# Linear attention and a gelu layer: the bf16 cast of v split between VectorE and ScalarE

## The chip, the cores and the metric

The kernel runs on one core of a Trainium2 chip. The metric is the device time of one execution in microseconds (us), the median of several runs. The core has five engines with a queue each: TensorE (PE in the profile, with PEld for its weight loads), VectorE (DVE), ScalarE (ACT), GpSimd (POOL) and SyncE (SP), which issues most DMA transfers. Each engine works through its own queue in order. They wait for one another through semaphores.

## The reference

Linear attention over 8 batches, 8 heads, 576 tokens and a head size of 64 makes a matrix of 4608 tokens by 512. This goes through two matrix products with a gelu between.

```python
def phi(x):
    return np.where(x > 0, x, np.exp(x) - 1.0) + 1.0
q_p, k_p = (phi(q), phi(k))
kv = np.einsum('bhsd,bhse->bhde', k_p, v)
z = np.sum(k_p, axis=2)
num = np.einsum('bhsd,bhde->bhse', q_p, kv)
den = np.einsum('bhsd,bhd->bhs', q_p, z)[..., None] + 1e-06
x = num / den                      # 4608 x 512 after moving the heads inside
h = x @ w_in                       # 512 -> 2048
g = 0.5 * h * (1.0 + np.tanh(c * (h + 0.044715 * h * h * h)))
out = g @ w_out                    # 2048 -> 512
```

All inputs and the output are float32. The kernel casts to bf16 for TensorE.

## The kernel before

The work goes batch by batch. For batch b there are these stages.

- k and v are loaded as `[128, 4, 9 * 64]`: a pair of heads `u` (four of them) fills the 128 partitions, 64 to a head, and each partition holds nine tokens, J = 9, of 64 values.
- `exp_of` (ScalarE, L219), `linear_of` (VectorE, L227) and `least_of` (VectorE, L233) compute phi of q and k in bf16 as the smaller of exp(x) and max(x + 1, 1).
- `cast_v_paired` (L237 to L241) casts v to bf16 into `vp`, in which the token `j` is outside the pair `u`, and each head's 64 values are followed by a one, so that the product with k gives the sum of k as a 65th column. Before the change it is one VectorE instruction for a whole batch (L238, 2304 elements a partition), and for batch 0 two, one for each half of the pairs.
- `kv_paired` (L243) multiplies k by v on TensorE: nine tokens, two pairs `s` and two head parities `a` make 36 small matmuls for one half of the pairs. `kv_evac` (L258) copies the sums out of PSUM into the block diagonal tile `kvbd`.
- `transpose_q` turns phi of q around on TensorE into PSUM (`t_ps`), and ScalarE copies it into `qts` (L430 in batch 0, L536 in batch 1). From batch 2 on a DMA does this.
- `nab` and its variants multiply q by `kvbd` (`n_ps`) and divide. The result x is transposed into `xt`.
- `h_mm` (L385) multiplies by `w_in`, `gelu` (L395) runs on ScalarE, and `o_mm` (L726) multiplies by `w_out`.

The pool is under a manual schedule, so each engine does its instructions in the order in which the code issues them. Batch 0 is written out in `first_batch`: the maps of q and k, the q transposes, the casts of v, and the two kv products, with `keep_warm` matmuls in between as filler for TensorE. The first product's sums lie in two banks of their own, one for each of two engines to copy; the second's lie in `pair_of_banks`, whose two banks are copied for one half of the partitions by VectorE and for the other by ScalarE (L451).

The attention of batch 1 is placed by `plan_second` into the steps of batch 0's gelu layer. `at(j, slot, fn)` queues a piece to be issued after step `slot` of batch j. The steps 0 to 15 of batch 0 are the sixteen blocks of h. Steps 16 to 35 are the output products, four tiles of tokens side by side over successive blocks of `w_out`. The pieces that matter here:

```python
at(0, 15, maps)
at(0, 23, transpose_q)
at(0, 23, casts)
at(0, 27, kv)
at(0, 27, last_w_out)
at(0, 29, n, 0)
```

Steps 24 to 27 are of two matmuls each, eight in all, and stand on TensorE between the transposes and the kv product. `maps` ends on ScalarE with a cast of half a block of `w_out`, `casts` does the other half on VectorE after v, and `last_w_out` casts the last block on GpSimd and ScalarE in turn.

PSUM is used through two pools: `ps_b` with six banks, from which `bank()` takes `h_ps`, `o_ps`, `t_ps` and batch 1's `kv_ps`, and `ps_a` with one pair of banks. The sum `o_ps` of each of the four token tiles of batch 0 is held from the first block to the last, that is from steps 16 to 19 up to steps 32 to 35.

Of the kernel before, what the change touches and what calls it, by code (L numbers as in the profile page):

```python
# [15 lines left out]
def kernel(  # L16
# [16 lines left out]
    nc = tc.nc  # L33

    B, H, S, D = q.shape
# [6 lines left out]
    NP = H // 2  # L42
    J = S // HP
    KM = d_model // P
    MM = d_ff // P
    E = D + 1
# [32 lines left out]
    def bank(name, shape, dt=FP32):  # L79
        return ps_b.tile(shape, dt, name=name, tag="b")  # L80

    def pair_of_banks(name):
        return ps_a.tile([P, 2, 512], FP32, name=name, tag="a")
# [3 lines left out]
    ld = {}  # L87
# [63 lines left out]
    halves = (slice(0, 2), slice(2, 4))  # L151
# [39 lines left out]
    def vp_paired(b):  # L191
        return vps[b % 2].rearrange("p (j u) e -> p j u e", u=NP)
# [19 lines left out]
    def exp_of(name, b, hs=None):  # L212
        x = ld[name, b]
        hs = hs or slice(0, x.shape[1])
        if (name, b) not in exps:
            e = name + ("_e" if name != "qr" or b % 2 else "_f")
            exps[name, b] = pe.tile([P, x.shape[2] // D, x.shape[1], D], BF16, name=e)
        o, i = maps_view(name, b, x, exps[name, b], hs)
        nc.scalar.activation(o, i, AF.Exp)  # L219

    def linear_of(name, b, hs=None):
        x = ld[name, b]
        hs = hs or slice(0, x.shape[1])
        if (name, b) not in phi:
            phi_tiles(name, b)
        o, i = maps_view(name, b, x, phi[name, b], hs)
        nc.vector.tensor_scalar(o, i, 1.0, 1.0, op0=ALU.add, op1=ALU.max)  # L227

    def least_of(name, b, hs=None):
        p, e = phi[name, b], exps[name, b]  # L230
        if hs:
            p, e = p[:, :, hs, :], e[:, :, hs, :]
        nc.vector.tensor_tensor(p, p, e, op=ALU.min)  # L233

    def cast_v_paired(b, us, fn):  # L237
        fn(  # L238
            out=vp_paired(b)[:, :, us, 0:D].rearrange("p j u d -> p u j d"),
            in_=ld["v", b][:, us].rearrange("p u (j d) -> p u j d", d=D),  # L240
        )  # L241

    def kv_paired(b, ii, kv_of):  # L243
# [14 lines left out]
    def kv_evac(b, blocks, src, *fns):  # L258
        for s in range(2):
            r = slice(HP * s, HP * (s + 1))  # L260
            fns[s % len(fns)](out=kvbds[b][r, blocks, E * s : E * (s + 1)], in_=src[r])  # L261
# [28 lines left out]
    def x_tile():  # L290
        return px.tile([P, d_model], BF16, name="x")
# [120 lines left out]
    def first_batch():  # L412
        w_ps = bank("w_ps", [P, 512])

        def keep_warm(n):
            for _ in range(n):
                nc.tensor.matmul(w_ps, lhsT=warm[:, 0:P], rhs=warm)  # L417

        qt = pt.tile([P, C, NP, P], BF16, name="qt")
        qs = (slice(0, 4), slice(4, 8))  # L420

        def transpose_q(s, fn):
            t_ps = bank("t_ps", [P, C, 2, P], BF16)
            for i in range(2):
                for c in range(C):
                    h = 4 * s + 2 * i
                    nc.tensor.transpose(
                        t_ps[:, c, i, :], phi["q", 0][:, c, h : h + 2, :], ident
                    )
            fn(out=qt[:, :, 2 * s : 2 * s + 2, :], in_=t_ps)  # L430

        keep_warm(18)
        for s in range(2):
            for n, hs in (("q", qs[s]), ("k", halves[s])):
                exp_of(n, 0, hs)
                linear_of(n, 0, hs)
                least_of(n, 0, hs)
        transpose_q(0, nc.scalar.copy)
        keep_warm(8)
        transpose_q(1, nc.scalar.copy)  # L440
        keep_warm(5)
        for ii in range(2):
            cast_v_paired(0, halves[ii], nc.vector.tensor_copy)
        kv_ps = [bank("kv_ps", [P, E]) for _ in range(2)]
        kv_paired(0, 0, lambda a, ii: kv_ps[a])
        for a, fn in enumerate((nc.vector.tensor_copy, nc.scalar.copy)):
            kv_evac(0, slice(2 * a, 2 * a + 1), kv_ps[a].rearrange("p (i e) -> p i e", i=1), fn)
        keep_warm(1)
        kv_ps = pair_of_banks("kv_ps")
        kv_paired(0, 1, lambda a, ii: kv_ps[:, a, 0:E])  # L450
        kv_evac(0, slice(1, 4, 2), kv_ps[:, :, 0:E], nc.vector.tensor_copy, nc.scalar.copy)  # L451
        for fs in (slice(0, 128), slice(128, 256), slice(256, 512)):
            cast_w_in(0, nc.gpsimd.tensor_copy, fs)
        cast_w_in(1, nc.gpsimd.tensor_copy, slice(256, 512))
        for i in range(2, 4):
            cast_w_in(i, nc.gpsimd.tensor_copy)
        for i in range(2):
            cast_w_out(i, nc.gpsimd.tensor_copy)

        xts[0] = pt.tile([P, NP, MAIN], BF16, name="xt")  # L460
        x = {0: x_tile()}

        def t(c, blocks=range(NP)):
            transpose_x(x[c], xt_chunk(0, c), nc.scalar.copy, blocks)

        def h(m, c, blocks=range(KM)):
            h_begin(0, m, slice(P * c, P * (c + 1)), blocks)

        first, second = range(2), range(2, 4)
        nab_half(x[0], qt[:, 0], 0)  # L470
        nab_half(x[0], qt[:, 0], 1)
        x[1] = nab(qt[:, 1], 0)
        t(0, first)
        h_begun[0][0] = bank("h_ps", [P, MAIN])
        nc.tensor.matmul(h_begun[0][0], lhsT=warm[:, 0:P], rhs=warm, skip_group_check=True)
        t(0, second)
        for m in range(2):
            h(m, 0, first)
        x[2] = nab_in_banks(qt[:, 2], 0)
        h(0, 0, second)  # L480
        t(1)
        h(1, 0, second)
        x[3] = nab(qt[:, 3], 0)
        cast_w_in(1, nc.vector.tensor_copy, slice(0, 256))
        h(2, 0)
        h(3, 0)
        t(2)
        for m in range(3):
            h(m, 1)
        t(3)  # L490
        gelu_table()
        h(3, 1)
        for c in (2, 3):
            for m in range(4):
                h(m, c)

    first_batch()


# [12 lines left out]
    def plan_second():  # L512
        b = 1
        x = {}

        def maps():
            for n in "qk":
                exp_of(n, b)
            cast_w_out(2, nc.scalar.copy, slice(0, 2))
            for n in "qk":  # L520
                linear_of(n, b)
            for n in "qk":
                least_of(n, b)

        def transpose_q():
            qts[b] = pt.tile([P, C, NP, P], BF16, name="qt")
            for s in range(2):
                t_ps = bank("t_ps", [P, 2, NP, P], BF16)
                for c in range(2):
                    for i in range(NP):  # L530
                        nc.tensor.transpose(  # L531
                            t_ps[:, c, i, :],
                            phi["q", b][:, 2 * s + c, 2 * i : 2 * i + 2, :],
                            ident,
                        )
                nc.scalar.copy(qts[b][:, 2 * s : 2 * s + 2], t_ps)  # L536

        def casts():
            cast_v_paired(b, slice(0, NP), nc.vector.tensor_copy)
            cast_w_out(2, nc.vector.tensor_copy, slice(2, 4))  # L540

        def kv():
            kv_ps = [bank("kv_ps", [P, 2, E]) for _ in range(2)]
            for ii in range(2):
                kv_paired(b, ii, lambda a, ii: kv_ps[a][:, ii, :])
            for a, fn in enumerate((nc.vector.tensor_copy, nc.scalar.copy)):
                kv_evac(b, slice(2 * a, 2 * a + 2), kv_ps[a], fn)

        def last_w_out():
            for m, fn in enumerate((nc.gpsimd.tensor_copy, nc.scalar.copy) * 2):  # L550
                cast_w_out(3, fn, slice(m, m + 1))
            gelu_table()

        def n(c):
            x[c] = (nab_in_banks if c == 1 else nab)(qts[b][:, c], b)

        def t(c):
            if c == 0:
                xts[b] = pt.tile([P, NP, MAIN], BF16, name="xt")
            transpose_x(x[c], xt_chunk(b, c), nc.scalar.copy)  # L560
# [7 lines that stand above are left out]
        at(0, 29, n, 1)  # L568
        at(0, 32, n, 2)
        at(0, 32, t, 0)  # L570
        at(0, 33, t, 1)
        at(0, 33, n, 3)
        at(0, 34, t, 2)
        at(0, 34.5, t, 3)
        at(0, 35, h_begin, b, 0, slice(0, 3 * P))
        at(0, 35, h_begin, b, 0, slice(3 * P, MAIN))
# [253 lines left out]
```

## Time and profile before

| what | value |
|---|---|
| time, median of 3 runs | 283.59 us (283.57 to 283.64) |
| span of the profiled execution | 281.8 us |
| TensorE busy | 276.0 us, 98% |
| ScalarE busy | 164.4 us, 58% |
| VectorE busy | 102.6 us, 36% |
| GpSimd busy | 15.0 us, 5% |
| casts of v on VectorE (L238), all batches | 9 instructions, 11.0 us |
| kv product of batch 0, second half | from 12.43 us |
| kv product of batch 1 | from 39.68 us |

The busy time of an engine is the sum of its instructions. The chain of waits follows the work that ended last back from the end, at each step to what released it. The timeline lists the instructions of each engine by their start, counted in us from the start of the span. In its rows, what stands in brackets is the idle time of that engine just before and what ended it. A group of equal instructions that follow one another is one row with a count; its duration runs from the first start to the last end.

### The profile page before, as it was taken

The page shows a single profiled execution, that of the slowest core. Times are in us where ns is not written, and L with a number is a line of the kernel's source. Part 1 is how long each engine was busy: PE and PEld are TensorE (multiplying, and loading weights), DVE is VectorE, ACT ScalarE, POOL GpSimd, SP SyncE. Part 2 cuts the span into 40 slices and gives each one's busy share as a digit, 9 for nine tenths or more (in the row PEclk, how much of TensorE's full clock was granted, in tenths as well). Part 3 has the DMA queues.
Part 4 walks back from the last instruction along what each step waited for, and adds up shares of the span by engine and source line. Part 5 has one row for each costly group of instructions (what it writes and reads, how often), then busy time and mean ns, then how long its engine had stood idle before and what let it go on. Part 6 is the DMA issues. An engine that isn't in the chain of part 4 may idle for free.

```text
span 281.8 us, 5145 instructions
## 1 busy us (share of the span) xinstructions
PE 276.0 (98%) x2181; PEld 134.9 (48%) x2181; DVE 102.6 (36%) x177; ACT 164.4 (58%) x224; POOL 15.0 (5%) x21
## 2 busy tenths in 40 slices
PE   8899999999999999999999999999999999999995
PEld 3574455445444544454445444544444444444444
DVE  3850386344955750356034640350124001400001
ACT  4678878785986915692569346833681364026400
POOL 3147210000000000000000000000000000000000
PEclk9999999999999999999999999999999999999999
DMA  6999999978999777906794630056405300420022
GB/s 244 400 406 397 411 401 404 404 256 218 190 367 296 267 170 214 370 24 172 201 385 101 161 120 2 2 149 169 93 2 149 111 2 0 131 94 0 0 77 74
DMA packets 59590, 53.81 MB, mean 191 GB/s; under 512 B 35760, under 2 KB 45360, under 8 KB 59568
## 3 DMA queue, kind: packets, MB, share of 16 engines
q1 hardware_dynamic: 56784, 44.58, 50.7%
q10 hardware_dynamic: 2784, 8.91, 8.9%
q8 instruction: 17, 0.28, 0.4%
q14 instruction: 5, 0.04, 0.0%
HBM read 36.70 MB, written 9.44 MB: 164 GB/s over the span
## 4 chain that ended last, share of the span: by engine, by line
PE 94%; DMA 3%; SPq 1%; DVE 1%; issue 0%; ACT 0%
PE o_ps L726 44%; PE h_ps L385 44%; DMA v_x<-in_v_dram 3%; PE n_ps L323 1%; PE n_ps L249 1%; PE kv_ps L249 1%; PE n_ps L265 1%; PE t_ps L378 1%; SPq L95 1%; SPq L100 0%; PE t_ps L531 0%; DVE vp L238 0%; DVE x L368 0%; DVE kvbd L261 0%; DVE o_sb L687 0%
## 5 line engine op out<-in xcount | busy, mean ns | idle before, releaser
L726 PE MATMUL o_ps<-w_out_sb,g 128*128 128x512 bf16 (+2 forms) x608 | 128.4, 368 | 0.0
L385 PE MATMUL h_ps<-xt,w_in_sb 128*128 128x512 bf16 (+1 forms) x564 | 113.7, 359 | 0.0
L395 ACT ACTIVATE g<-h_ps 128x512 bf16<-128x512 f32 x144 | 84.6, 599 | 36.3 <-PE h_ps L385 35.1
L385 PEld LDWEIGHTS <-w_in_sb 128*128 128x128 bf16 x628 | 58.5, 98 | 64.6
L726 PEld LDWEIGHTS <-g 128*128 128x128 bf16 x608 | 57.4, 98 | 63.5
L687 ACT COPY o_sb<-o_ps 128x512 f32<-128x512 f32 (+1 forms) x19 | 10.8, 576 | 65.4 <-PE o_ps L726 58.6
L687 DVE COPY o_sb<-o_ps 128x512 f32<-128x512 f32 (+1 forms) x19 | 12.2, 645 | 50.4 <-PE o_ps L726 45.5
L282 DVE RECIPROCAL r<-n_ps 128x6 f32<-128x6 f32 (+2 forms) x43 | 8.2, 191 | 61.3 <-PE n_ps L323 55.8
L227 DVE TENSOR_SCALAR k_p<-k_x 128x2304 bf16<-128x2304 f32 (+1 forms) x9 | 11.0, 1222 | 24.1 <-DMA k_x<-in_k_dram 24.1
L283 DVE TENSOR_TENSOR xs<-n_ps,r 128x384 bf16<-128x384 f32 (+1 forms) x30 | 17.5, 584 | 1.0
L219 ACT ACTIVATE k_e<-k_x 128x2304 bf16<-128x2304 f32 (+1 forms) x9 | 17.1, 1903 | 0.9 <-DMA k_x<-in_k_dram 0.8
L219 ACT ACTIVATE q_e<-q_x 128x2048 bf16<-128x2048 f32 (+1 forms) x9 | 15.5, 1719 | 2.8 <-DMA q_x<-in_q_dram 2.7
L227 DVE TENSOR_SCALAR q_p<-q_x 128x2048 bf16<-128x2048 f32 (+1 forms) x9 | 9.9, 1102 | 13.0 <-DMA q_x<-in_q_dram 13.0
L385 PE MATMUL h_ps<-xt_rest,w_in_sb 128*128 128x512 bf16 x64 | 14.0, 379 | 0.0
L233 DVE TENSOR_TENSOR q_p<-q_p,q_e 128x2048 bf16<-128x2048 bf16 (+1 forms) x9 | 9.9, 1099 | 6.9 <-ACT q_e L219 6.8
L408 ACT ACT_TABLE_LOAD x9 | 11.5, 1283 | 0.2
L233 DVE TENSOR_TENSOR k_p<-k_p,k_e 128x2304 bf16<-128x2304 bf16 (+1 forms) x9 | 11.0, 1221 | 1.2 <-ACT k_e L219 1.0
L238 DVE CAST vp<-v_x 128x2304 bf16<-128x2304 f32 (+1 forms) x9 | 11.0, 1222 | 0.5 <-DMA v_x<-in_v_dram 0.4
L417 PE MATMUL w_ps<-warm 128*128 128x512 bf16 x32 | 9.7, 459 | 1.2 <-DVE warm L181 1.2
L219 ACT ACT_TABLE_LOAD x8 | 10.3, 1283 | 0.1
L139 POOL CAST w_in_sb<-w_st 128x512 bf16<-128x512 f32 (+2 forms) x6 | 7.6, 1270 | 14.7 <-DMA w_st<-in_moe_w_in_dram 14.7
L283 DVE TENSOR_TENSOR x<-n_ps,r 128x512 bf16<-128x512 f32 (+1 forms) x13 | 7.9, 609 | 0.4
(50 smaller groups left out, 75.9 us busy)
## 6 DMA issues: line engine op xcount, KB each, us to landing
out_dram<-o_sb ACTq DMA_DIRECT2D x16, 512.0 KB, 3.8
k_x<-in_k_dram SPq DMA_DIRECT2D x7, 1152.0 KB, 7.0
v_x<-in_v_dram SPq DMA_DIRECT2D x7, 1152.0 KB, 12.0
q_x<-in_q_dram SPq DMA_DIRECT2D x6, 1024.0 KB, 11.8
w_st<-in_moe_w_in_dram SPq DMA_DIRECT2D x3, 1024.0 KB, 13.5
q_x<-in_q_dram SPq DMA_DIRECT2D x4, 512.0 KB, 8.4
w_st<-in_moe_w_out_dram SPq DMA_DIRECT2D x2, 1024.0 KB, 12.5
w_st<-in_moe_w_out_dram SPq DMA_DIRECT2D x4, 512.0 KB, 11.2
```

The source lines that it names most:

```text
L219: nc.scalar.activation(o, i, AF.Exp)
L227: nc.vector.tensor_scalar(o, i, 1.0, 1.0, op0=ALU.add, op1=ALU.max)
L233: nc.vector.tensor_tensor(p, p, e, op=ALU.min)
L238: fn(out=vp_paired(b)[:, :, us, 0:D].rearrange("p j u d -> p u j d"), in_=ld["v", b][:, us].rearrange("p u (j d) -> p u j d", d=D),)
L282: nc.vector.reciprocal(r, n_v[heads + (D,)])
L283: nc.vector.tensor_tensor(x_v, n_v[heads + (slice(0, D),)], r[heads + (None,)].to_broadcast(shape + [D]), op=ALU.mult,)
L385: nc.tensor.matmul(h_ps[:, ts], lhsT=w_in_sb[:, c, P * m : P * (m + 1)], rhs=xt[:, c, ts], start=(c == 0), stop=(c == KM - 1), skip_group_ ...
L395: nc.scalar.activation(g[:, m, :], h_ps, AF.Gelu_apprx_tanh)
L408: nc.scalar.preload_act_table_set("gelu_apprx_tanh_and_others")
L417: nc.tensor.matmul(w_ps, lhsT=warm[:, 0:P], rhs=warm)
L687: (nc.scalar.copy if on_scalar else nc.vector.tensor_copy)(dst, src)
L726: nc.tensor.matmul(o_ps, lhsT=g[:, m, P * t : P * (t + 1)], rhs=w_out_sb[:, m, fs], start=(m == 0), stop=(m == MM - 1),)
```

## The change

`cast_v_paired` gets a parameter `js`, the tokens that it casts. In batch 0 the second half of v, and in batch 1 all of v, is cast in two parts: tokens 0 to 5 by VectorE and 6 to 8 by ScalarE. In batch 1 ScalarE's part is issued between its two copies of the transposed q. In addition, both copies of batch 0's second kv product are issued to ScalarE, where VectorE did one of them. What it is for: v lands late in both batches, TensorE's product needs all of it, and two engines share the cast.

```diff
-    def cast_v_paired(b, us, fn):
+    def cast_v_paired(b, us, fn, js=slice(0, J)):
         fn(
-            out=vp_paired(b)[:, :, us, 0:D].rearrange("p j u d -> p u j d"),
-            in_=ld["v", b][:, us].rearrange("p u (j d) -> p u j d", d=D),
+            out=vp_paired(b)[:, js, us, 0:D].rearrange("p j u d -> p u j d"),
+            in_=ld["v", b][:, us].rearrange("p u (j d) -> p u j d", d=D)[:, :, js],
         )
...
-        for ii in range(2):
-            cast_v_paired(0, halves[ii], nc.vector.tensor_copy)
+        cast_v_paired(0, halves[0], nc.vector.tensor_copy)
+        cast_v_paired(0, halves[1], nc.vector.tensor_copy, slice(0, 6))
+        cast_v_paired(0, halves[1], nc.scalar.copy, slice(6, J))
...
-        kv_evac(0, slice(1, 4, 2), kv_ps[:, :, 0:E], nc.vector.tensor_copy, nc.scalar.copy)
+        kv_evac(0, slice(1, 4, 2), kv_ps[:, :, 0:E], nc.scalar.copy)
...
                 nc.scalar.copy(qts[b][:, 2 * s : 2 * s + 2], t_ps)
+                if s == 0:
+                    cast_v_paired(b, slice(0, NP), nc.scalar.copy, slice(6, J))
 
         def casts():
-            cast_v_paired(b, slice(0, NP), nc.vector.tensor_copy)
+            cast_v_paired(b, slice(0, NP), nc.vector.tensor_copy, slice(0, 6))
             cast_w_out(2, nc.vector.tensor_copy, slice(2, 4))
```

## The prediction

> **What bounds the kernel now.** I read the page first, then the chain of waits in order of time, then the timeline of the two stretches in which batch 0's and batch 1's v are cast.
>
> ```profile
> PE 276.0 (98%) x2181; PEld 134.9 (48%) x2181; DVE 102.6 (36%) x177; ACT 164.4 (58%) x224; POOL 15.0 (5%) x21
> ```
>
> TensorE (PE) is busy for 98% of the span, so time can only come from, or go into, the few places where it waits. The chain of waits shows that from about 13.6 us to the last store it is TensorE with hardly a break. Before that comes this (start us, us, what):
>
> ```profile
> 3.36 8.23 DMA v_x<-in_v_dram
> 11.59 0.02 issue
> 11.61 0.77 DVE vp L238
> 12.39 0.04 issue
> 12.43 0.52 PE kv_ps L249 x33
> 12.94 0.02 issue
> 12.97 0.30 DVE kvbd L261
> 13.27 0.02 issue
> 13.29 0.27 ACT kvbd L261
> 13.56 0.04 issue
> 13.60 0.29 PE n_ps L359 x2
> ```
>
> The load of v's second half lands at 11.59, VectorE (DVE) casts it, TensorE multiplies, VectorE copies one half of the result, then ScalarE (ACT) the other half, one after the other, and only then does TensorE go on. Each of these links is touched by the change. Batch 1 has its own v cast in the same chain, further on:
>
> ```profile
> 37.11 0.89 PE t_ps L531 x16
> 38.01 1.73 PE o_ps L726 x8
> 39.73 0.73 PE kv_ps L249 x72
> ```
>
> Here TensorE does not wait: the eight output products lead into the kv product without a gap. How close it is, the timeline shows (start us, us, engine, line, operation):
>
> ```profile
> 34.10 1.36 DVE L227 TENSOR_SCALAR k_p<-k_x 128x2304 bf16<-128x2304 f32 x1 [4.18 <-DMA k_x<-in_k_dram]
> ...
> 36.19 1.03 ACT L145 CAST w_out_sb<-w_st 128x1024 bf16<-128x1024 f32 x1
> 36.51 1.35 DVE L233 TENSOR_TENSOR k_p<-k_p,k_e 128x2304 bf16<-128x2304 bf16 x1
> ...
> 36.95 1.06 PE L531 MATMUL t_ps<-ident,q_p 128*128 128x128 bf16 x16
> 37.60 1.93 ACT L536 COPY qt<-t_ps 128x1024 bf16<-128x1024 bf16 x2 [0.38 <-PE t_ps L531]
> ...
> 38.26 1.36 DVE L238 CAST vp<-v_x 128x2304 bf16<-128x2304 f32 x1 [0.40 <-DMA v_x<-in_v_dram]
> ...
> 39.55 0.69 DVE L145 CAST w_out_sb<-w_st 128x1024 bf16<-128x1024 f32 x1
> 39.68 0.67 PEld L249 LDWEIGHTS <-k_p 64*64 64x64 bf16 x72 [0.44 <-DVE vp L238]
> ```
>
> Two things end just ahead of the kv product at 39.68: VectorE's cast of v at 38.26 + 1.36 = 39.62, and ScalarE's second copy of the transposed q at 37.60 + 1.93 = 39.53. The second counts through PSUM: `ps_b` has six banks, four hold the open `o_ps` sums of batch 0 (allocated at slots 16 to 19, finished from slot 32 on), so the two `kv_ps` banks of `kv()` can only be the two `t_ps` banks of `transpose_q`, and both must have been read out by ScalarE. The first matmul of `kv_paired` writes one of them and the second the other, so the product can't get going before the later copy is done. The wait view names nobody who waits for L536, because it is over 0.09 us ahead of the cast.
>
> **What the Trainium skill says.** "ScalarE: Activation LUTs", What ACT_TABLE_LOAD costs, prices an activation with immediate operands at 186 ns + 0.833 ns an element, and lets neighbours overlap by about 93 ns. The trace agrees: ScalarE's f32 casts of 512 and 1024 elements took 617 and 1029 ns (the formula gives 613 and 1039), and the two qt copies of 1012 and 1018 ns took 1.93 us together, an overlap of 0.10. "VectorE: DVE Perf Modes", The perf-mode tier table, has an f32 copy in SBUF at two elements a cycle; the casts of 1152 and 2304 elements, 762 and 1362 ns, are 0.52 ns an element plus 0.16 us, which agrees. "PSUM — Partial Sum Buffer", PSUM bank collisions raise a hardware error, says that the chip doesn't arbitrate two engines on one bank and that the order is software's to make. The trace fits: in the pair of banks at 12.97 ScalarE began 0.02 us after VectorE had ended, while in the first half, with a bank for each engine, they overlap (12.19 and 12.29).
>
> **Part 1, batch 0's second half of v.** VectorE now casts 6 x 2 x 64 = 768 elements: 762 - 384 x 0.52 = 0.56 us, from 11.61 to 12.17 in place of 12.38. ScalarE casts 384: 186 + 320 = 0.51 us. It is free when its second qt copy ends (9.87 + 1.91 = 11.78, with overlap from 11.69), the load has landed at 11.59, so it runs 11.70 to 12.21. TensorE is held by the filler matmul until about 12.2 and then by VectorE's part, so kv starts at 12.23 in place of 12.43; tokens 6 to 8 come after 24 of its 36 matmuls, at about 12.55, so ScalarE's part is hidden. Behind that cast stand ScalarE's copies of the first half (12.19 to 12.62 before), now 12.19 at the earliest, so nothing is lost. Gain 0.20 us.
>
> **Part 2, both copies of that product by ScalarE.** Before: 12.97 to 13.56, with a handover. After: kv ends 0.2 earlier, ScalarE starts at 12.77 and, going by its pair of 64x130 copies at 40.60 (0.54 us for two), ends at 13.31; `n_ps` follows at 13.36 in place of 13.60. VectorE's reciprocal is freed, but waits for TensorE anyway. Gain of parts 1 and 2 together: 0.24 us. w_in's first casts on GpSimd end at 14.17 and 15.41, ahead of their products (14.73 and 16.04, less 0.24), so TensorE keeps this gain up to the q transposes of batch 1.
>
> **Part 3, batch 1.** VectorE's cast shrinks from 2304 to 1536 elements: 1.36 - 768 x 0.52 = 0.96 us, so its part of vp is there at 39.22. ScalarE gets 768 elements, 186 + 640 = 0.83 us, and they stand between its two qt copies, so the second copy is queued behind them. Step by step:
> - VectorE's map of k waits for a load (4.18 us of idle before 34.10), which the change doesn't move; so q's last map, ahead of the 36.51 row, still ends near 36.6, and the transposes can come forward only from 36.95 to about 36.75.
> - First qt copy: 37.60 - 0.20 = 37.40, on to 38.41. ScalarE is free for it (its w_out cast ends at 37.22).
> - Cast: from 37.40 + 0.91 = 38.31, just after the load landed (38.26), to 39.14.
> - Second qt copy: with 0.09 overlap from 39.05, to 40.06.
> - kv: 40.06 + 0.05 = 40.11, against 39.68 before. TensorE, which would be there at 39.73 - 0.24 = 39.49, stands for 0.6 us; queued behind are the output products, `nab` and everything after.
>
> So the kv product ends 0.38 to 0.43 us later than before, take 0.40. Its copies (40.59 to 41.19) hide behind four output products both times. ScalarE's later casts wait for loads (42.06) and have room; I find no slack in TensorE from 40.5 to 47.6 to take the delay up: the chain's pieces there are 24 x 0.216 + 32 x 0.056 + kv = 7.7 of 7.84 us, so at most 0.15 could be absorbed. From there on all is TensorE-bound. VectorE's w_out cast moves up by 0.4 us unless its load holds it; TensorE isn't waiting for it. Sum: 283.59 + 0.40 = 283.99 us.
>
> Costs not in the trace: a ScalarE cast of 384 or 768 f32 elements in runs of 192 each. From below, the 512 and 1024 rows' line gives 0.51 and 0.82; from above, the exp of 1024 with a reordered output (1.06) adds 0.03. I take the line. VectorE's new shape may cost 0.1 us more; it hides behind ScalarE in batch 1 and takes 0.1 from part 1.
>
> **The rivals.**
> - The bank wait doesn't bind, and only vp counts. For it: no row of the wait view shows anybody waiting for L536. Then kv follows TensorE at 39.49, as both parts of vp are there in time (39.22, and 39.14 for the tokens used last), and the gain of the first stage stays: 283.59 - 0.24 = 283.35. Against it: the six banks leave no others. Some wait elsewhere that hides the delay would give about the same.
> - Slower by over 0.2%. The first stage's gain doesn't reach ScalarE's row (transposes held by VectorE's maps at 36.95 as now) and the cast does not overlap: the copy starts at 37.60, the cast at 38.51 + 0.10, the second copy at 39.44 to 40.45, kv at 40.50, which is 0.82 late: 284.4. With overlap it is 40.31, 0.63 late: 284.22. For it: the q maps at 36.6 sit close to the transposes.
> - Faster by over 0.2%, that is by 0.57 us. Stage one's whole handover is 0.24, and the loosest spots up to 47.6 hold 0.15 more: 283.2. It would need an effect that I don't see.
>
> **How the numbers follow.** ScalarE's longer row binds, and the delay is 0.2 to 0.57: 0.50. The larger delay, 284.2 to 284.4: 0.30. The small gain about 283.35: 0.12. Faster than 283.0: 0.08. So faster 0.08, same 0.50 + 0.12 = 0.62, slower 0.30. The range runs from the small gain to most of the larger delay, 283.3 to 284.35, and leaves out the faster case and the tail above, under 0.2 together.
>
> **What would show it.** In the changed profile: kv of batch 0 near 12.23 and `n_ps` L359 near 13.36 (parts 1, 2); ScalarE's row copy, cast, copy from 37.4 to 40.06; TensorE idle for about 0.6 us ahead of kv at 40.1, put down to ACT qt L536; VectorE's vp cast over by 39.2. A kv near 39.5 would make the bank argument wrong; one at 40.3 or later would mean that the first gain died before it; a delay at 40.1 that is gone at 47.6 would mean slack that I missed.

## The result and the profile after

The changed kernel takes 285.65 us (285.58 to 285.72, six executions) against 283.58 us (283.52 to 283.73): the ratio is 1.0073, with an interval of 1.006 to 1.0086. It is 2.07 us slower, where 0.40 was forecast. The span of the profiled execution grew from 281.8 to 283.9 us, and TensorE's busy time hardly (276.0 to 276.1), so the time went into waits of TensorE:

```profile
PE 276.1 (97%) x2181; PEld 134.7 (47%) x2181; DVE 101.9 (36%) x176; ACT 165.4 (58%) x227; POOL 15.0 (5%) x21
```

I read the chain of waits of the changed kernel in order of time (start us, us, what), beside that of before. First the stretch of batch 0's second kv half:

```profile
10.81 0.69 DVE vp L238
...
11.54 0.48 PE kv_ps L249 x36
12.02 0.32 PE w_ps L417
12.34 0.45 PE kv_ps L249 x36
12.79 0.02 issue
12.81 0.27 ACT kvbd L261
13.08 0.01 issue
13.09 0.27 ACT kvbd L261
13.37 0.04 issue
13.41 0.29 PE n_ps L359 x2
```

The row at 10.81 is the cast of v's first half. The cast of the second half, from 11.59 to 12.15 on VectorE, no longer stands in the chain: TensorE comes from the first half's product and the filler matmul (`w_ps`), and the second product follows that at 12.27 by the timeline. So the filler is now the limit, and a cast that is faster still would bring nothing here. Both copies are ScalarE's, and `n_ps` starts at 13.41 in place of 13.60. That is 0.19 us gained between these two executions. In both the loads landed at nearly the same time; in other executions with nothing changed at the start they come up to 0.4 us later (experiment 4). Counted from the start of the first half's product, which takes the loads out, `n_ps` follows after 1.87 us in place of 2.04, so the gain is 0.17. Then batch 1's cast, in the timeline of the changed kernel:

```profile
36.75 1.06 PE L532 MATMUL t_ps<-ident,q_p 128*128 128x128 bf16 x16
37.40 1.01 ACT L537 COPY qt<-t_ps 128x1024 bf16<-128x1024 bf16 x1 [0.23 <-PE t_ps L532]
...
38.14 0.96 DVE L238 CAST vp<-v_x 128x1536 bf16<-128x1536 f32 x1 [0.34 <-DMA v_x<-in_v_dram]
38.31 0.85 ACT L238 CAST vp<-v_x 128x768 bf16<-128x768 f32 x1
...
39.05 1.01 ACT L537 COPY qt<-t_ps 128x1024 bf16<-128x1024 bf16 x1
...
39.47 0.21 PE L249 MATMUL kv_ps<-vp,k_p 64*64 64x65 bf16 x1
...
40.11 0.77 PE L249 MATMUL kv_ps<-vp,k_p 64*64 64x65 bf16 x71 [0.43 <-ACT qt L537]
```

The first of the 72 matmuls goes at 39.47, into the bank that is free; the other 71 stand until ScalarE's second copy has read out the other bank, and start at 40.11, where 39.68 was the start before. From here the chain of waits is 0.42 us late: the h products that follow on it begin at 47.99 and not at 47.57. So far all is as forecast. What comes next is not. The chain of the changed kernel goes on:

```profile
47.99 2.62 PE h_ps L385 x16
50.60 0.02 issue
50.63 0.61 ACT g L395
51.23 3.27 ACTq L718
...
55.04 2.56 ACT g L395 x5
57.60 0.02 issue
57.62 1.28 ACT L219
58.90 0.01 issue
58.91 1.91 ACT q_e L219
60.82 2.02 ACT k_e L219
62.84 0.02 issue
62.87 1.37 DVE k_p L233
64.24 0.04 issue
64.28 0.78 PE kv_ps L249 x72
```

and the same stretch of before:

```profile
47.57 6.92 PE h_ps L385 x36
54.49 6.91 PE o_ps L726 x32
61.40 0.86 PE h_ps L385 x4
62.26 0.71 PE kv_ps L249 x72
```

Before, the chain stays on TensorE. After, it leaves TensorE at 50.6 for ScalarE's queue ("ACTq"): L718 is the store of batch 0's output tiles, two tiles to a store and two stores, each a DMA that ScalarE issues between gelus. The change doesn't touch it (it was L715 before). The timeline of ScalarE has it in the kernel before as

```profile
50.27 1.17 ACTq L715 DMA_DIRECT2D out_dram<-o_sb  x2
51.49 1.09 ACT L395 ACTIVATE g<-h_ps 128x512 bf16<-128x512 f32 x2 [0.68 <-PE h_ps L385]
```

and in the changed one as

```profile
50.63 4.36 ACTq L718 DMA_DIRECT2D out_dram<-o_sb  x2
55.04 2.56 ACT L395 ACTIVATE g<-h_ps 128x512 bf16<-128x512 f32 x5 [3.82 <-PE h_ps L385]
```

The first of the two issues takes 3.87 us (0.39 before), and from 51.23, when the gelu that began with it ends, ScalarE does nothing else: five gelus are piled up at 55.04. Behind them stand the exps of the next q and k, on which the maps of k on VectorE wait, and on those the kv product of batch 2. The rows of before that this is measured against are

```profile
56.44 1.91 ACT L219 ACTIVATE q_e<-q_x 128x2048 bf16<-128x2048 f32 x1
...
60.39 1.36 DVE L233 TENSOR_TENSOR k_p<-k_p,k_e 128x2304 bf16<-128x2304 bf16 x1 [0.79 <-ACT k_e L219]
```

The sum closes: the exps start at 58.91 and not at 56.44, 2.47 us late; before, k's map ended at 60.39 + 1.36 = 61.75, 0.51 us ahead of the product at 62.26; 2.47 - 0.51 = 1.96, and the product is at 64.28, 2.02 late. Of this 0.42 was there already at 47.99, so the store's issue costs about 1.6 us, and it stays to the end.

I call an issue that takes 2 us or more *held*. The question is why this store is held by a change that touches neither it nor its neighbours. Ahead of it ScalarE does two instructions more than before in batch 0 (a cast and one of the copies) and one more in batch 1.

### The profile page after: what moved, and what is told of

The parts are those of the page before. It is cut to its first block, busy times and chain, and to the rows that moved or that the text cites. A ratio compares the mean times of both kernels' runs of the same rounds, so it can differ in the third digit from the quotient of the medians.

```text
span 283.9 us, 5145 instructions
## 1 busy us (share of the span) xinstructions
PE 276.1 (97%) x2181; PEld 134.7 (47%) x2181; DVE 101.9 (36%) x176; ACT 165.4 (58%) x227; POOL 15.0 (5%) x21
## 4 chain that ended last, share of the span: by engine, by line
PE 88%; ACT 4%; DVE 2%; DMA 2%; ACTq 1%; issue 0%; SPq 0%; DVEq 0%
PE h_ps L385 42%; PE o_ps L729 41%; DMA k_x<-in_k_dram 2%; PE n_ps L323 1%; ACTq L718 1%; ACT k_e L219 1%; PE kv_ps L249 1%; ACT g L395 1%; DVE k_p L233 1%; PE n_ps L249 1%; PE n_ps L265 1%; ACT qt L537 1%; PE t_ps L378 1%; ACT q_e L219 1%; ACT L219 0%
## 5 line engine op out<-in xcount | busy, mean ns | idle before, releaser
L238 DVE CAST vp<-v_x 128x2304 bf16<-128x2304 f32 (+3 forms) x9 | 10.4, 1156 | 0.4 <-DMA v_x<-in_v_dram 0.3
```

Source lines behind the costliest of these rows:

```text
L238: fn(out=vp_paired(b)[:, js, us, 0:D].rearrange("p j u d -> p u j d"), in_=ld["v", b][:, us].rearrange("p u (j d) -> p u j d", d=D)[:, :, js],
```

## The experiments

In all of them the kernel before took 283.76 to 283.80 us in the same sessions. Ratios are to it, with their intervals. A *place* is the number of ScalarE's records that the trace has ahead of the first store, waits on semaphores counted: 61 in the kernel before, 63 in the changed one. It is not the number of instructions alone, since an instruction more can save a wait: the changed kernel has three instructions more there, and its place is two higher.

**1. Parts 1 and 2 alone** (batch 1 as before).

```diff
-                if s == 0:
-                    cast_v_paired(b, slice(0, NP), nc.scalar.copy, slice(6, J))
...
-            cast_v_paired(b, slice(0, NP), nc.vector.tensor_copy, slice(0, 6))
+            cast_v_paired(b, slice(0, NP), nc.vector.tensor_copy)
```

> Batch 0's parts alone (v's second half split, both copies on ScalarE); batch 1 as before. Both theories: batch 0's kv product and n_ps come 0.2 us earlier as in the changed kernel, but batch 1's kv waits for VectorE's whole cast, which waits for the load (38.26 + 1.36), so kv stays at 39.7 and the time is 283.5 to 283.6. ScalarE's store of batch 0 stays near 50.25 and takes 0.4 us to issue.

Measured: 286.65 us, ratio 1.0102 (1.0087 to 1.0117). Both theories had 283.6 at most, and neither came true. The store was held for 4.75 us, at place 63, and batch 2's kv product started at 65.38. So the hold doesn't need part 3, nor the wait for the bank: batch 1's kv product starts at 39.96 with all 72 matmuls at once. That is 0.28 later than in the kernel before, because the loads landed later in this execution; whether the hour matters is for experiments 2 and 4.

**2. Part 3 alone** (batch 0 as before).

```diff
-        cast_v_paired(0, halves[0], nc.vector.tensor_copy)
-        cast_v_paired(0, halves[1], nc.vector.tensor_copy, slice(0, 6))
-        cast_v_paired(0, halves[1], nc.scalar.copy, slice(6, J))
+        for ii in range(2):
+            cast_v_paired(0, halves[ii], nc.vector.tensor_copy)
...
-        kv_evac(0, slice(1, 4, 2), kv_ps[:, :, 0:E], nc.scalar.copy)
+        kv_evac(0, slice(1, 4, 2), kv_ps[:, :, 0:E], nc.vector.tensor_copy, nc.scalar.copy)
```

> Batch 1's split alone. Bank theory: kv at 40.1 to 40.3, a gain of nothing before it. Theory A (the store is blocked because it comes later than about 50.6): blocked for 3 to 4 us, time 285.6 to 285.9. Theory B (the blocking has nothing to do with when the store comes but with the altered queue of ScalarE): the same. If the store is not blocked the time is 284.0 to 284.2.

Measured: 284.4 us, 1.0023 (1.0014 to 1.0031). The store took 0.38 us, at place 61: not held. It came at 50.88, and in experiment 1 a store at 50.87 was held, so the hour doesn't decide. The time is 0.2 us over what was expected for a store that isn't held. The timeline shows the bank's wait alone, in the size of the second rival with overlap (0.63 us, and 284.4 - 283.77 = 0.63):

```profile
39.71 0.21 PE L249 MATMUL kv_ps<-vp,k_p 64*64 64x65 bf16 x1
...
40.35 0.77 PE L249 MATMUL kv_ps<-vp,k_p 64*64 64x65 bf16 x71 [0.43 <-ACT qt L536]
```

**3. The changed kernel, its stores one gelu earlier.**

```diff
-                at(1, 2, store)
+                at(1, 1, store)
```

> The changed kernel with batch 0's stores issued one gelu earlier, after step 1 in place of step 2 of batch 1, so at about 49.8 in place of 50.7. Theory A (the time of the issue decides): the issue takes 0.4 us, kv still at 40.1, time 284.0, as predicted for the change. Theory B (the altered queue decides): blocked all the same, 285.6 or more.

Measured: 284.23 us, 1.0017 (1.001 to 1.0025). Place 62, issue 0.39 us at 49.99. Nothing held, and the time is 0.46 over before: close to the 0.40 that was forecast for the change.

**4. The kernel before, its stores one gelu later.**

```diff
-                at(1, 2, store)
+                at(1, 3, store)
```

> The kernel before with batch 0's stores issued one gelu later, after step 3 of batch 1, so at about 51.1 in place of 50.27; nothing else changed. Theory A (the time decides): blocked until about 54.5, so some 3.4 us, and 1.2 to 1.7 us slower, 284.8 to 285.3. Theory B (the altered queue decides): 283.6.

Measured: 283.83 us, 1.0001 (0.9993 to 1.001). The first store came at 51.51, later than in the changed kernel (50.63), at place 62, and took 0.38 us. The late hour alone is not the cause.

**5 to 7. Instructions without effect, into a new tile.** One such copy in the changed kernel, one and two in the kernel before.

```diff
+    pad = const.tile([P, 8], BF16, name="pad")
+    for i in range(1):
+        nc.scalar.copy(pad[:, i : i + 1], warm[:, 0:1])
```

> The changed kernel with one tiny ScalarE copy (128x1) put at the start, where ScalarE waits for the first load anyway. Batch 0's first store moves from place 63 to place 64 in ScalarE's queue, its time does not move. Theory P1 (the store is blocked when it stands at place 63 exactly, a boundary at which ScalarE's next instructions are fetched): issue 0.4 us, time 284.0 to 284.2. Theory P2 (blocked from place 63 on, until the fetch has come): blocked, 285.6. Theory T (blocked in a narrow window of time, just when batch 2's v has landed at about 50.7): blocked, 285.6.

> The same with one tiny copy: the first store at place 62. All theories: not blocked, 283.6. If it is slower, the tiny copies cost something by themselves.

> The kernel before with two such tiny copies at the start: the first store moves from place 61 to 63, and stays at about 50.3. Theories P1 and P2: blocked for 3 to 5 us, time 285 to 287. Theory T: 283.6.

Measured, in the order of the three texts: 288.39 us (1.0162, 1.0147 to 1.0178), held for 4.20 us at place 64; 285.91 (1.0076, 1.0061 to 1.0091), not held, place 62; 289.33 (1.0195, 1.018 to 1.0211), held for 5.30 us at place 63. One copy in the kernel before cost 2.1 us without any hold: the new tile of 16 bytes a partition stands ahead of others, and the loads came later (batch 1's v cast began at 40.56, not 38.26, after a wait for its load). It is the tile and not the copy: by the packet records, the load packets of 2048 and 2304 bytes in the first 30 us took 91.6 to 91.7 ns in the mean in these three kernels, and 87.0 to 87.7 in all others, experiment 8 with its two copies among them (87.0). So these three mix two things. The step from one copy to two, 3.4 us with place 62 turned into 63, pointed at the place; a cleaner test is next.

**8. Two instructions without effect, and no tile moved.** The copies go into spare columns of a tile that is there.

```diff
-    ident = const.tile([P, P + 64], BF16, name="ident")[:, 0:P]
+    ident_t = const.tile([P, P + 64], BF16, name="ident")
+    ident = ident_t[:, 0:P]
...
+    for i in range(2):
+        nc.scalar.copy(ident_t[:, P + i : P + i + 1], warm[:, 0:1])
```

> The kernel before with two tiny ScalarE copies (128x1) at the start, this time into spare columns of a tile that is there already, so that no other tile moves in memory. The first store goes from place 61 to place 63 of ScalarE's queue and stays near 50.3. Place theory (first store of ScalarE blocked from place 63 on): blocked for 3 to 5 us, time 285.2 to 286.7, and the start as in the kernel before. Theory M (what made the padded kernels slow was only the moved tiles, and the blocking goes with the time): 283.6.

Measured: 286.89 us, 1.0109 (1.0094 to 1.0124). ScalarE's timeline:

```profile
50.87 5.25 ACTq L718 DMA_DIRECT2D out_dram<-o_sb  x2
56.16 2.06 ACT L398 ACTIVATE g<-h_ps 128x512 bf16<-128x512 f32 x4 [5.08 <-issue]
```

The kernel before, with two copies of one element a partition ahead of everything, is 3.1 us slower, and its store is held for 4.77 us. No cast of v, no copy of kv and no bank has changed. Of the 3.1 us, about 0.3 were there before the store: the h products start at 47.85 and not at 47.57, as v landed later in this execution (in that of experiment 4, which has no such copies, the start is 0.4 late). The rest, about 2.8, comes with the hold. Two more instructions ahead of the store on ScalarE are enough to bring it.

**9. The changed kernel with a small transfer by ScalarE at the start.**

```diff
...
+    nc.scalar.dma_start(out=ident_t[:, P : P + 32], in_=warm[:, 0:32])
```

> The changed kernel with a tiny transfer (128x32 bf16 from SBUF to spare columns in SBUF) issued by ScalarE at the start. The first store of batch 0 is then ScalarE's second transfer and stands at place 64. Theory F (only the first transfer that ScalarE issues can be blocked, from place 63 on): issue 0.4 us, time 284.0 to 284.2. Theory G (any store that comes while ScalarE's next instructions are being fetched): blocked, 285.5 or more.

Measured: 286.09 us, 1.0079 (1.0062 to 1.0096), held for 3.78 us at place 64. The early transfer took 0.55 us to issue. That the store is ScalarE's first DMA is not the reason. The start is late here too (`n_ps` at 13.98, not 13.41), so the whole time is no measure of the hold.

**10 and 11. The changed kernel, its stores two and five gelus later.** As in 3, with `at(1, 4, store)` and `at(1, 7, store)`.

> The changed kernel with the stores two gelus later, place 66 in ScalarE's queue, at about 52.4. Theory H (a store is held only while ScalarE's next block of instructions is on its way, from about place 63 until some 3.5 us later): held from 52.4 to about 54.5, so some 2 us; time 284.2 to 285. Theory R (any place from 63 on, whatever the time): held 4 us, 285.5 or more. Theory N (only places 63 and 64): not held, 284.1.

> The changed kernel with the stores five gelus later, place 74, at about 55. Theory H: the block has come by then, not held, 284.0 to 284.2. Theory R: held, 285.5 or more. Theory N: not held.

Measured: two later, 284.9 us (1.0035, 1.0021 to 1.0049), issued at 52.47, place 66, held for only 2.00 us; five later, 284.25 us (1.0017, 1.0008 to 1.0025), issued at 55.46, place 71 (74 was expected; that is the second store's), 0.38 us. So a late place doesn't hold a store at every hour. The hold seems to end at something, whenever the store came, as theory H had it.

**12. The changed kernel, batch 0's stores issued by SyncE.**

```diff
-                nc.scalar.dma_start(out=ov, in_=o_sb)
+                (nc.sync if j == 0 else nc.scalar).dma_start(out=ov, in_=o_sb)
```

> The changed kernel with batch 0's two stores issued by SyncE, which has nothing else to issue between 48.9 and 60 us. ScalarE goes on with its gelus whatever happens to the store. All theories: the delay of batch 1's kv is left, 284.0 to 284.2; slower than that only if the moved store holds up the loads behind it.

Measured: 284.2 us, 1.0015 (1.0008 to 1.0021). ScalarE's gelus go through without a stop in the stretch in which they stood (its timeline):

```profile
50.83 0.60 ACT L395 ACTIVATE g<-h_ps 128x512 bf16<-128x512 f32 x1 [0.27 <-PE h_ps L385]
51.70 0.60 ACT L395 ACTIVATE g<-h_ps 128x512 bf16<-128x512 f32 x1 [0.27 <-PE h_ps L385]
...
53.42 0.60 ACT L395 ACTIVATE g<-h_ps 128x512 bf16<-128x512 f32 x1 [0.27 <-PE h_ps L385]
```

So ScalarE could work on between 51 and 55; only a DMA issue of its own was held. Over the kernel before in the same session this version is 284.20 - 283.80 = 0.40 us slower, the changed kernel in its own session 2.07: the hold's price is 1.67 us, and 0.40 is the rest of the change.

**What the hold ends at.** In the DMA view of the changed kernel, cut to 52 to 53 us, two packets of another kind, "instruction", stand among the loads:

```profile
q8 instruction: 1, 0.02, 5.9%
q14 instruction: 1, 0.01, 2.0%
```

The one on queue q14 is 8192 bytes, the one on q8 16384. The table follows the q14 packet. Worked out from the packet records and ScalarE's records of each trace, in the page's us (issue and packet are starts; "after" is the end of the issue less the packet's start; "no." is the experiment):

```
no.  kernel                    place  issue   took  packet  after
 15  own_banks_dve               60   50.34   0.38   54.79      -
  -  before                      61   50.27   0.39   54.59      -
  2  second_batch_only           61   50.88   0.38   55.09      -
 16  t_pair_slot1                62   49.56   0.38   53.67      -
 14  own_banks_slot1             62   49.80   0.39   53.87      -
  3  after_store_slot1           62   49.99   0.39   54.04      -
 13  first_batch_slot1           62   49.50   0.38   53.61      -
  4  before_store_slot3          62   51.51   0.38   55.75      -
  6  before_pad1                 62   52.58   0.38   56.92      -
  -  changed                     63   50.63   3.87   52.74   1.76
  1  first_batch_only            63   50.87   4.75   54.06   1.56
  8  before_spare2               63   50.87   4.77   54.11   1.53
  7  before_pad2                 63   52.94   5.30   56.44   1.80
  5  after_pad1                  64   52.84   4.20   55.19   1.85
  9  after_early_dma             64   51.21   3.78   53.25   1.74
 10  after_store_slot4           66   52.47   2.00   52.75   1.72
 11  after_store_slot7           71   55.46   0.38   52.90      -
```

In all seven held runs the issue ends 1.5 to 1.9 us after that packet begins, whether the hold took 2.0 or 5.3 us; the one first store at a late place that was not held came 2.6 us after the packet. The q8 packet fits less well: in the same seven runs the issue ends 1.9 to 3.3 us after it. The packet's time goes with the store, too: in the changed kernel with no store of ScalarE's ahead of it (experiments 11 and 12) the packet begins at 52.90 and 52.92, with both stores ahead of it (experiment 3) at 54.04. The reading that fits all first stores: the packet brings ScalarE's next block of instructions, that block was still on its way through DMA engines full of loads (8 tenths busy or more in every slice from 50.6 to 54.6 in the changed kernel's DMA view, 399 GB/s in the mean), and a DMA issue from the far side of the border waited for it. This is an inference from the packet's kind and its time, not shown: no run took the loads away or moved the packet by itself. And one thing speaks against so simple a rule: the second store of the kernels that were not held, 0.5 to 0.8 us after the first, mostly stood at place 63 or 64, 3.2 to 3.5 us ahead of the packet, and was not held either. Why these went through stays open.

**13. Parts 1 and 2 alone, stores one gelu earlier** (1 and 3 together), to see what they bring without the hold.

> Batch 0's parts alone, with the stores after step 1 of batch 1 (place 62). Place theory: not blocked, so 283.5 to 283.7 in place of 286.65: kv of batch 1 waits for VectorE's whole cast and stays at 39.7, which swallows the 0.2 us of the start. If the 2.9 us of that kernel came from batch 0's parts themselves: 286.

Measured: 283.78 us, 0.9999 (0.9991 to 1.0008); place 62, not held. The time alone can't tell a gain of 0.17 us from none. The trace shows where it goes: batch 1's kv product starts at 39.77, right after VectorE's cast of v (38.35 + 1.36 = 39.71), and that cast waits for a load which nothing has moved.

**14 to 16. Can part 3 be mended?** Two versions give batch 1's kv product the separate pair of banks, with the copies on two engines (stores one gelu earlier) or both on VectorE; the third puts the transposed q there.

```diff
-            kv_ps = [bank("kv_ps", [P, 2, E]) for _ in range(2)]
+            kv_ps = pair_of_banks("kv_ps")
+            kv_v = [kv_ps[:, a, 0 : 2 * E].rearrange("p (i e) -> p i e", e=E) for a in range(2)]
...
```

> The changed kernel, with batch 1's kv product in the separate pair of banks of the other pool, so that it no longer waits for ScalarE's second qt copy, and with the stores after step 1 (place 62). Bank theory: kv follows the output products at 39.5, 0.2 before the kernel before, and the time is 283.3 to 283.45. If something else than the banks held kv at 40.1: 284.0 as with the stores moved alone.

Measured: 284.22 us, 1.0015 (1.0007 to 1.0022), a miss in time, though kv comes when it was expected. The timeline:

```profile
39.50 0.78 PE L249 MATMUL kv_ps<-vp,k_p 64*64 64x65 bf16 x72
...
40.41 0.60 DVE L261 CAST kvbd<-kv_ps 64x130 bf16<-64x130 f32 x2 [0.18 <-PE kv_ps L249]
...
41.12 0.54 ACT L261 CAST kvbd<-kv_ps 64x130 bf16<-64x130 f32 x2 [1.03 <-DVE kvbd L261]
...
41.71 0.51 PE L265 MATMUL n_ps<-kvbd,qt 128*128 128x130 bf16 x6 [0.40 <-ACT kvbd L261]
```

The product no longer waits for ScalarE's second copy and starts at 39.50, all 72 matmuls at once: the shared bank was the cause of its wait. But the two engines now copy out of one tile of two banks, one after the other, and `n_ps` waits for the second; the gain is handed back 2 us later. Each engine has a bank of its own here and they still take turns, so the turns are not the banks' doing; as the wait in the row of 41.12 suggests, the program orders copies by two engines out of one tile. The prediction put the turns at 12.97 and 13.29 in the kernel before down to the banks; there, too, both copies come out of one such tile.

```diff
-            kv_ps = [bank("kv_ps", [P, 2, E]) for _ in range(2)]
...
-            for a, fn in enumerate((nc.vector.tensor_copy, nc.scalar.copy)):
-                kv_evac(b, slice(2 * a, 2 * a + 2), kv_ps[a], fn)
+            kv_in_pair(b)
```

> The changed kernel with batch 1's kv product in the separate pair of banks and both of its copies by VectorE (as batch 2 has them). ScalarE's queue is two instructions and a wait shorter, so the store stands at place 60, at about 50. Bank theory: kv at 39.5, its copies 40.4 to 41.2, n_ps at 41.3, stores not blocked, time 283.35 to 283.55, so below the kernel before. If the copies on VectorE take longer than four output products, n_ps goes to 41.5 or later and the gain is gone.

Measured: 283.85 us, 1.0003 (0.9994 to 1.0011), a miss. The store stood at place 60 and was not held, but there is no gain:

```profile
39.54 0.78 PE L249 MATMUL kv_ps<-vp,k_p 64*64 64x65 bf16 x72
...
40.46 0.87 DVE L657 CAST kvbd<-kv_ps 64x260 bf16<-64x260 f32 x2 [0.21 <-PE kv_ps L249]
...
41.38 0.64 PE L265 MATMUL n_ps<-kvbd,qt 128*128 128x130 bf16 x8
```

Two copies by one engine last 0.87 us, two engines side by side took 0.60 in the kernel before (40.59 to 41.19). So `n_ps` follows the kv product's start by 1.84 us in place of 1.59, which eats the gain.

```diff
+            t_ps = ps_a.tile([P, 2, 2, NP, P], BF16, name="t_ps", tag="a")
...
-                t_ps = bank("t_ps", [P, 2, NP, P], BF16)
...
-                nc.scalar.copy(qts[b][:, 2 * s : 2 * s + 2], t_ps)
+            for s in range(2):
+                nc.scalar.copy(qts[b][:, 2 * s : 2 * s + 2], t_ps[:, s])
```

> A version meant to keep the gain: the changed kernel with batch 1's two transposes of q in the pair of banks (all sixteen ahead of the first copy), so that the kv product has two free banks and its copies go side by side as before, and with the stores after step 1 (place 62). Bank theory: kv at 39.5, n_ps at 41.15 in place of 41.27, stores not held: 0.1 to 0.25 us below the kernel before. If the first qt copy comes so late that ScalarE's copies of kv wait behind its second one: no gain, 283.7 to 284.0.

Measured: 283.71 us, 0.9994 (0.9986 to 1.0002). It is the best of the changed kernels, and not to be told from the kernel before; the gain of 0.1 to 0.25 us that was hoped for is neither shown nor excluded. No version beat the kernel before clear of the noise.

## Why the prediction failed

- **Parts 1 and 2: right.** kv of batch 0's second half at 12.27 (forecast 12.23), ScalarE's cast 0.53 us (0.51), `n_ps` at 13.41 (13.36); the gain was 0.17 to 0.19, not 0.24. The transposes of batch 1's q came forward to 36.75, as forecast. What the gain is worth alone at the end is not shown (experiment 13).
- **Part 3: right to 0.01 us in this execution.** ScalarE's row at 37.40, 38.31, 39.05 as written, the cast 0.85 (forecast 0.83), VectorE's 0.96 (0.96), the product at 40.11 (40.11). The sizes and the order are what was foreseen; that the times agree so closely is partly luck, since the loads landed as in the trace of before. In experiment 3 the same row comes 0.23 us later (the product at 40.34). The argument on the six banks held: experiment 14 took the shared banks away and the product came at 39.50, where the first rival had 39.49. That rival falls only because the banks are in fact shared.
- **"I find no slack in TensorE from 40.5 to 47.6": right.** The delay was 0.42 at 47.99, and 0.40 and 0.46 us of time in the two versions in which the store is not held (12 and 3).
- **"From there on all is TensorE-bound. Sum: 283.59 + 0.40 = 283.99 us": here it failed.** The change also added instructions to ScalarE's queue, and the step took it that after 47.6 no engine but TensorE could set the time. The issue of ScalarE's own stores was put at nothing, without a word. In the run, ScalarE's first store is held for 3.87 us, TensorE waits for batch 2's maps, and about 1.6 us (2.02 - 0.42 by the chain, 2.07 - 0.40 by experiment 12) come on top of the 0.42. Experiment 8 shows the cause without anything else of the change: two copies of no use bring the hold, and +3.1 us. Experiments 3 and 12 take it away again by the store alone.
- **The rivals.** The second, with its delay of 0.63 us, is right for part 3 alone (experiment 2); for the whole change it named the right side for another reason. None of the cases looked at the issue times of ScalarE's own DMAs, though the profile before showed the stores in ScalarE's queue in the middle of the gelus, so the range ended at 284.35.

What is settled: the bank's wait and its size, that two more ScalarE instructions ahead of the store bring the hold, and that issuing the store one gelu earlier or from SyncE takes it away. What is not: the mechanism of the hold beyond its end 1.5 to 1.9 us after an instruction packet, whether it needs the loads beside it, and why second stores at the same places pass.

## What to carry to other kernels

A change that adds instructions to a compute engine also moves every DMA which that engine issues to a later place in its queue. Look at the issue times of such DMAs in the timeline after each change (0.39 against 3.87 us here), and if one is long, give it to an engine that has nothing else to do, or move it by a step, before judging the change: here that was 1.67 us of 2.07.

When work is put between two copies out of PSUM, ask who waits for the second one's bank, even if the wait view names nobody; and where a kernel waits for a load, casting faster what has landed brings only what the next wait leaves of it (0.17 to 0.19 us here, and at 39.8 the next load decides again).

## What was not expected of the hardware

- The issue of the first store on ScalarE took 2.0 to 5.3 us in seven kernels and 0.38 to 0.39 in the others where ScalarE issues it. Once the gelu before it has ended, ScalarE executes nothing in that time, while without an issue of its own it went on through the same stretch (experiment 12).
- Two ScalarE copies of 128x1 at the very start made the kernel 3.1 us slower (1.0109), about 2.8 of it with the hold.
- A new tile of 16 bytes a partition, with one such copy, cost 2.1 us without a hold (1.0076): with it batch 1's v was there 2.3 us later (its cast began at 40.56, not 38.26). Load packets of 2048 and 2304 bytes took 91.7 ns in the mean in place of 87.0. What in the tiles' new places slows them wasn't tried.
